# Opening a fused kernel with one unit's inverse instead of two, weight splits in 16 groups, and joint layers parted by weight halves

## The chip, the cores and the metric

The kernel runs on one core of a Trainium2 chip. The metric is device time in microseconds of one execution. The engines of a core run their own instruction streams in order and wait for each other by semaphores: TensorE (PE, with its weight loads shown apart as PEld), VectorE (DVE), ScalarE (ACT), GpSimd (POOL) and SyncE (SP), whose queue issues most of the DMAs.

## The reference

Two things are computed one after the other. For 4 batches x 8 heads, a delta-rule attention over 768 steps with head size 48, and then a feed-forward layer with a squared ReLU on the 3072 x 384 result:

```python
for t in range(S):
    y[:, :, t] = np.einsum('bhd,bhde->bhe', q[:, :, t], state)
    v_old = np.einsum('bhde,bhd->bhe', state, kt)       # kt: normalized k of step t
    state = state + bt[:, :, :, None] * np.einsum('bhd,bhe->bhde', kt, vt - v_old)
...
h = np.maximum(x @ w_in, 0.0)                           # w_in 384 x 2048
return (h * h @ w_out).astype(np.float32)               # w_out 2048 x 384
```

The weights arrive as 64-bit floats, two 32-bit words for each.

## The kernel before, in words

The work is cut into 12 units of 128 time steps x 2 batches (`units`). A unit's attention is blocked: two chunks of 64 steps, of which each needs the inverse of a triangular matrix. For most units that inverse is made on VectorE by `invert` (32 steps of two operations, L363 and L366, on blocks brought there through DRAM by the DMAs of L328 and L335), and goes back through DRAM into `tt` (L375 to L384). `static` (L280) does transposes (L301) and products (L311) with masks (L320); `whole`, `applied` (L592) and `sequential` (L616) do the rest of a unit's attention. Its output `y` is fed to the layers by `feed` (L662) as a high and a low part.

`layers` (L694) takes the 2048 hidden columns in 8 pairs (`fp`) per unit of 256 tokens: two halves of 9 matmuls (L735), the activation on ScalarE (L742 to L745), a subtraction for the low part on VectorE (L704), and later two halves of 6 matmuls (L717). A generator `yield`s after each half, so a unit's layers are 32 steps and a few more.

Every weight must first be turned from a 64-bit float into two float32r parts: `fetch` loads it, `split_weights` scales the upper word on ScalarE (L147) and combines the words by six VectorE operations (L154 to L171), or, in the first `SUMS` parts, by four operations and three matmuls (`low`, L177). There are 28 parts: 12 of `w_in` with 512 columns and 16 of `w_out` with 384, in the order of use. The working tiles come from `spool`'s `a` and `rest` with two buffers, and from `mpool`'s.

Units 0 and 1 are opened together by `first_pair` (L386): beta through `betas` and `sides`, blocks next to the diagonal by `near`, a solve of 15 double steps on VectorE for both units at once (`solve`, L472 to L505), and then products on PE that join the halves (`inner`, `joined`, `outer`, `last`). The order of instructions is written out by hand (`manual_schedule`): first this opening with pieces of the splits in between, then for each u from 1 to 11 a period, in which `weave` merges generators by given fractions of the period: `loads` (for unit u + 2: k, q, beta, normalization; for u + 1: v), `static` of unit u + 1, `state_part` of unit u, `invert` of unit u + 1, and the layers of unit u - 1. The layers of units 0 and 1 are one generator, `joint`: first half of the weights for unit 0, both halves for unit 1, second half for unit 0; unit 0's partial sums wait in `kept`, a buffer of `vt`. Of its steps, 50 lie in period 1 and the rest in period 2.

Of the kernel before, what the change touches and what calls it, by code (L numbers as in the profile page):

```python
# [20 lines left out]
def kernel(  # L21
# [25 lines left out]
    P = 128  # L47
# [28 lines left out]
    eye = spool.tile([P, 512], F32, name="a")[:, :P]  # L76
# [19 lines left out]
    ttile = []  # L96

    def new_tt():
        tt = apool.tile([P, NU, NC, H, C], F32, name="tt", bufs=1)
        ttile[:] = [tt[:, i] for i in range(NU)]  # L100
        return tt
# [13 lines left out]
    EACH = PC // P  # L115
    weight_parts = []
    for part in range(DF // PC):
        weight_parts += [("wi", (kt, part), w_in[kt * P:(kt + 1) * P, part * PC:(part + 1) * PC]) for kt in range(KT)]
        weight_parts += [("wo", ft, w_out[ft * P:(ft + 1) * P]) for ft in range(part * EACH, (part + 1) * EACH)]
    NW = len(weight_parts)  # L120
    place = [f"w{x}" for x in range(NW)]
    raws = []
    halves = {}

    rooms = [(spool, "a", "rest"), (mpool, "r", "h_l")]
    AHEAD, SUMS = 10, 6

    def fetch(n):
        for _ in range(n):
            x = len(raws)  # L130
            if x < NW:
                src = weight_parts[x][2]
                raw = wpool.tile([P, src.shape[1], 2], I32, name=place[x])
                nc.sync.dma_start(out=raw.rearrange("p a b -> p (a b)"), in_=src.bitcast(I32))
                raws.append(raw)

    def split_weights():
        started = []

        def begin():  # L140

            x = len(started)
            if x < NW:
                n = raws[x].shape[1]
                pool, first, second = rooms[x % 2 if x < AHEAD else 0]
                a, rest = [pool.tile([P, PC], I32, name=name)[:, :n] for name in (first, second)]
                nc.scalar.activation(out=a.bitcast(F32), in_=raws[x][:, :, 1].bitcast(F32), func=AF.Abs, scale=DOWN)  # L147
                started.append((a, rest))

        def words(x, sums):  # L150
            a, rest = started[x]
            n = a.shape[1]
            w0, w1 = [raws[x][:, :, i] for i in range(2)]
            nc.vector.tensor_scalar(out=a, in0=a, scalar1=3, scalar2=0 if sums else 1,  # L154
# [3 lines left out]
            if sums:  # L158
# [3 lines left out]
                hl = wpool.tile([P, 2, n], F32R, name=place[x])  # L162
            else:
# [4 lines left out]
                hl = wpool.tile([P, 2, n], F32R, name=place[x])  # L168
                power = apool.tile([P, PC], I32, name="t1", bufs=1)[:, :n]
# [3 lines left out]
            nc.scalar.copy(out=hl[:, 0], in_=a.bitcast(F32))  # L173
            halves[weight_parts[x][:2]] = hl[:, 0], hl[:, 1]
            return a, rest, hl

        def low(a, rest, hl):  # L177
            turn[1] += 1
            ps = ps_o.tile([P, PC], F32, name=f"o{turn[1] % 2}")[:, :hl.shape[2]]
            nc.tensor.matmul(ps, lhsT=ident, rhs=a.bitcast(F32), start=True, stop=False)  # L180
            nc.tensor.matmul(ps, lhsT=minus, rhs=hl[:, 0], start=False, stop=False)
            nc.tensor.matmul(ps, lhsT=plus, rhs=rest.bitcast(F32R), start=False, stop=True)
            nc.scalar.copy(out=hl[:, 1], in_=ps)

        before = None
        begin()
        begin()
        yield
        for x in range(NW):
            sums = x < SUMS  # L190
            now = words(x, sums)
            if before:
                low(*before)
            before = now if sums else None
            if x + 2 < AHEAD:
                begin()
            if x >= AHEAD - 3:
                yield
            if x + 2 >= AHEAD:
                begin()  # L200
            yield

# [14 lines left out]
    def load(u):  # L217
        t0, b0 = (u // NU) * P, (u % NU) * 2
        d = dict(u=u, t0=t0, b0=b0, y=[None] * NC, marks={})
        d["kp"] = kpad[u % 3]  # L220
        load_to(d["kp"], k, d, D, (nc.sync, nc.scalar) if u <= 1 else None)
        return d
# [21 lines left out]
    def normalize(*ds):  # L244
# [4 lines left out]
        for i in range(n):  # L249
            for c in range(NC):  # L250
                h = slice(c * H, (c + 1) * H)

                sq = (apool.tile([P, H, D], F32, name="r", bufs=2) if ds[0]["u"] in (2, 3) else
                      spool.tile([P, PC], F32, name="rest")[:, :H * D].rearrange("p (h e) -> p h e", h=H))
# [18 lines left out]
    def x_tile(u=2):  # L273

        turn[0] += 1
        pool, name = (ps_h, "h") if u <= 1 and turn[0] % 4 >= 2 else (ps_x, "x")
# [69 lines left out]
    def invert(d):  # L346
# [22 lines left out]
        if d["u"] == 2:  # L369
            tt = new_tt()  # L370
            for rows in (slice(HB, C), slice(C + HB, P)):
                nc.gpsimd.memset(tt[rows, :, :, :, :HB], 0.0)
# [3 lines left out]
        rows = ttile[d["u"] % 2].rearrange("p c h t -> p (c h) t")  # L376
# [9 lines left out]
    def first_pair(ds):  # L386


        HS = HB // 2
        NX = NC * NP  # L390
        quarter = [slice(n * HB, (n + 1) * HB) for n in range(4)]
        upper, lower = quarter[::2], quarter[1::2]
        chs = [(c, 2 * p + j, j, c * NP + p) for c in range(NC) for p in range(NP) for j in range(2)]
        made, ttall = {}, new_tt()

        def unit(i, t):
            return ttall[:, i, :, :, t].rearrange("p c h t -> p (c h) t")

        def betas():
            raw = apool.tile([P, P], F32, name="tmp", bufs=1)  # L400
            for j in range(2):
                for i, d in enumerate(ds):
                    at = (j * 2 + i) * NX
                    for r in range(2):
                        src = beta[d["b0"] + (r ^ j), j::2, d["t0"]:d["t0"] + P].rearrange("p (c t) -> c p t", c=NC)
                        nc.gpsimd.dma_start(out=raw[at:at + NX, r * C:(r + 1) * C], in_=src)
            for d in ds:
                d["kq"] = apool.tile([P, NC, NP, 2, 2, C], F32, name="kq", bufs=2)
                d["ap"] = apool.tile([P, NC, H, 2, C], F32, name="ap", bufs=2)
            z = apool.tile([P, 2, HS, HS], F32, name="z", bufs=1)  # L410
            nc.gpsimd.memset(z, 0.0)
            nc.gpsimd.affine_select(out=z, in_=z, pattern=[[0, 2], [1, HS], [-1, HS]], base=0, channel_multiplier=0,
                                    compare_op=ALU.not_equal, fill=1.0)
            made.update(raw=raw, z=z)

        def sides():
            flat = apool.tile([P, 2, 2 * NX, 2], F32, name="b0", bufs=1)
            across = apool.tile([P, 2, 2, HS], F32, name="b1", bufs=1)
            bt = apool.tile([P, 2, HS], F32, name="btp", bufs=1)
            out_ = apool.tile([P, 2, 2, HS], F32, name="sides", bufs=1)  # L420
            ps = ps_g.tile([P, 2, PC], F32, name="g")[:, 0, :HB]
            nc.tensor.transpose(ps, made["raw"][:HB], ident[:HB, :HB])
            nc.scalar.copy(out=flat, in_=ps.rearrange("p (j x) -> p j x", j=2).unsqueeze(3).broadcast_to(list(flat.shape)))
            yield
            nc.vector.transpose(out=across.rearrange("p j e s -> p (j e s)"), in_=flat.rearrange("p j x e -> p (j x e)"))
            nc.vector.tensor_scalar(out=bt, in0=across[:, :, 0], scalar1=parity[:, 0:1], scalar2=None, op0=ALU.mult)
            nc.vector.scalar_tensor_tensor(out=bt, in0=across[:, :, 1], scalar=parity[:, 1:2], op0=ALU.mult, op1=ALU.add,
                                           in1=bt)
            for e in range(2):
                nc.vector.tensor_scalar(out=out_[:, e], in0=bt, scalar1=parity[:, e:e + 1], scalar2=None, op0=ALU.mult)  # L430
            made.update(bt=bt, sides=out_)
            yield

        def transposed(i, which):
            d = ds[i]
            for c in range(NC):
                tp = x_tile(0).rearrange("p (n t) -> p n t", n=NP)
                for p in range(NP):
                    src = d["qp" if which else "kp"][:, c, 2 * p:2 * p + 2]
                    nc.tensor.transpose(tp[:, p], src.rearrange("p a b -> p (a b)"), ident)  # L440
                nc.scalar.copy(out=d["kq"][:, c, :, :, which], in_=tp.rearrange("p n (b t) -> p n b t", b=2))

        def near(i):

# [532 lines left out]
```

## Time and profile before

| | |
|---|---|
| median of 3 runs | 703.14 us (702.07 to 704.07) |
| profiled execution | 701.87 us, span 700.1 us |
| mean granted TensorE clock | 0.930 |
| PE busy | 627.3 us, 90% of the span |
| PE weight loads | 591.9 us, 85% |
| VectorE busy | 437.3 us, 62% |
| ScalarE busy | 327.6 us, 47% |
| GpSimd busy | 38.9 us, 6% |
| DMA | 47.67 MB, mean 68 GB/s |

Busy times are means over stages that have different limits, so the shares alone do not name the bound. The rows below give the engine's name, the line of the kernel, the operation, the tile written and the tiles read, and times in us from the start of the span; `SPq` is time in the issue queue of SP.

### The profile page before, as it was taken

To read this page: it belongs to the slowest core of one execution; us is meant where nothing else is said; L and a number is where in the kernel's file an instruction comes from. 1 tells how busy PE (TensorE), PEld (TensorE's weight loads), DVE (VectorE), ACT (ScalarE), POOL (GpSimd) and SP (SyncE) were. 2 spreads that over 40 slices of the span, in tenths; PEclk is the share of its full clock that TensorE was granted. 3 is DMA by queue.
4 is the path that set the end of the run, shared out by engine and by line. 5 is a ranking of instruction groups with operands and counts; after the bars stand their busy time and mean duration, and the time that the engine had idled before them with its cause. 6 is when DMAs were issued, how large, how long until landed. Compare 5 with 4: busy or idle time off the path is not lost.

```text
span 700.1 us, 24612 instructions
## 1 busy us (share of the span) xinstructions
PE 627.3 (90%) x10657; PEld 591.9 (85%) x10657; DVE 437.3 (62%) x1193; ACT 327.6 (47%) x606; POOL 38.9 (6%) x65
## 2 busy tenths in 40 slices
PE   2729759789784999999999999999999999999997
PEld 2527749788773899999999999999999999999997
DVE  5777777899476359367477576494684774651211
ACT  4705636545331454454544545535535445354352
POOL 5002300001100100100101001001001000000000
PEclk9955658989996899999999999999999999999999
DMA  7893200320332341441532423414415315020100
GB/s 181 269 365 60 38 2 2 71 44 1 54 77 47 66 87 29 91 78 28 104 59 34 99 49 46 101 34 74 90 20 111 65 23 102 11 49 16 23 2 23
DMA packets 163692, 47.67 MB, mean 68 GB/s; under 512 B 155632, under 2 KB 158720, under 8 KB 163584
## 3 DMA queue, kind: packets, MB, share of 16 engines
q1 hardware_dynamic: 160992, 45.48, 30.8%
q8 instruction: 84, 1.38, 0.8%
q10 hardware_dynamic: 2336, 0.59, 0.4%
q14 instruction: 24, 0.20, 0.1%
q0 software_dynamic: 256, 0.02, 0.0%
HBM read 36.01 MB, written 9.96 MB: 66 GB/s over the span
## 4 chain that ended last, share of the span: by engine, by line
PE 73%; DVE 14%; SPq 5%; issue 3%; DMA 2%; ACT 2%; DVEq 0%; ACTq 0%
PE h L735 27%; PE o L717 26%; SPq L215 4%; PE g L633 3%; PE g L609 2%; DVE tmp L363 2%; DVE z L366 2%; PE x L301 2%; PE x L646 2%; PE g L301 2%; PE x L311 1%; PE x L602 1%; PE g L311 1%; PE g L654 1%; DVE rest L166 1%
## 5 line engine op out<-in xcount | busy, mean ns | idle before, releaser
L717 PE MATMUL o<-w,h_h 128*128 128x384 f32 x768 | 203.6, 346 | 6.4 <-ACT vt L763 6.4
L735 PE MATMUL h<-x_h,w 128*128 128x256 f32 x1056 | 160.4, 288 | 1.5 <-ACT x_h L670 0.9
L704 DVE TENSOR_TENSOR h_l<-r,h_h 128x512 fp32r<-128x512 f32 x96 | 66.2, 689 | 141.7 <-PE o L717 67.7
L735 PEld LDWEIGHTS h<-x_h,w 128*128 128x128 f32 x1056 | 141.6, 191 | 6.9 <-issue 1.8
L717 PEld LDWEIGHTS o<-w,h_h 128*128 128x128 f32 x768 | 133.4, 190 | 8.9 <-ACT vt L763 6.6
L742 ACT ACTIVATE r<-h 128x512 f32<-128x512 f32 x96 | 57.4, 598 | 164.9 <-PE h L735 158.4
L717 PE MATMUL o<-w,h_l 128*128 128x384 f32 x384 | 130.3, 339 | 1.3 <-DVE h_l L704 1.3
L363 DVE SCALAR_TENSOR_TENSOR tmp<-lt,bt,z 128x126 f32<-128x126 f32 (+22 forms) x310 | 95.7, 309 | 29.2 <-DMA lt<-blocks 11.8
L735 PE MATMUL h<-x_l,w 128*128 128x256 f32 x528 | 91.6, 282 | 0.0
L366 DVE TENSOR_TENSOR z<-z,tmp 128x126 f32<-128x126 f32 (+22 forms) x310 | 79.2, 256 | 10.6
L735 PEld LDWEIGHTS h<-x_l,w 128*128 128x128 f32 x528 | 75.7, 191 | 0.0
L717 PEld LDWEIGHTS o<-w,h_l 128*128 128x128 f32 x384 | 72.8, 190 | 2.2 <-DVE h_l L704 2.2
L743 ACT ACTIVATE r<-r 128x512 f32<-128x512 f32 x96 | 60.8, 633 | 3.1
L745 ACT CAST h_h<-r 128x512 fp32r<-128x512 f32 x96 | 59.7, 622 | 3.1
L633 PEld LDWEIGHTS g<-state,kq 48*64 48x64 f32 x1408 | 23.5, 138 | 8.7 <-issue 2.8
L633 PE MATMUL g<-state,kq 48*64 48x48 f32 x1408 | 26.2, 224 | 4.5 <-DVE state L649 2.4
L173 ACT CAST w<-a 128x384 fp32r<-128x384 f32 (+1 forms) x23 | 12.8, 556 | 35.0 <-DVE rest L166 34.0
L588 ACT ACTIVATE tt<-x 32x256 f32<-32x256 f32 x40 | 15.0, 376 | 26.1 <-PE x L584 25.6
L354 POOL MEMSET z<- 128x512 f32 x10 | 5.4, 536 | 391.5 <-DMA inv<-z 391.4
L609 PE MATMUL g<-vt,tt 64*64 64x48 f32 x768 | 26.4, 225 | 0.3 <-ACT y L657 0.2
L609 PEld LDWEIGHTS g<-vt,tt 64*64 64x64 f32 x768 | 25.5, 142 | 0.5 <-ACT y L657 0.3
L256 DVE TENSOR_REDUCE n<-rest 128x8 f32<-128x384 f32 x20 | 10.9, 549 | 24.0 <-ACT rest L255 24.0
(193 smaller groups left out, 766.5 us busy)
## 6 DMA issues: line engine op xcount, KB each, us to landing
w<-in_moe_w_in_dram SPq DMA_DIRECT2D x12, 512.0 KB
w<-in_moe_w_out_dram SPq DMA_DIRECT2D x16, 384.0 KB
lt<-blocks SPq DMA_DIRECT2D x20, 256.0 KB
vt<-in_v_dram SPq DMA_DIRECT2D x96, 48.0 KB
kpad<-in_k_dram SPq DMA_DIRECT2D x88, 48.0 KB
qpad<-in_q_dram SPq DMA_DIRECT2D x88, 48.0 KB
out_dram<-a SPq DMA_DIRECT2D x42, 96.0 KB
blocks<-ap SPq DMA_DIRECT2D x40, 64.0 KB
```

Of the source, the lines that this page charges most:

```text
L215: queue.dma_start(out=dst[rows, c, j::2, :width], in_=src[:, c, j::2])
L301: nc.tensor.transpose(tp[:, p], src[:, c, 2 * p:2 * p + 2].rearrange("p a b -> p (a b)"), ident)
L363: nc.vector.scalar_tensor_tensor(out=tmp, in0=lt[:, s:s + 1, s + 1:].broadcast_to([P, nj, nt]), scalar=bt[:, s:s + 1], op0=ALU.mult, op1=A ...
L366: nc.vector.tensor_tensor(out=z[:, :nj, s + 1:], in0=z[:, :nj, s + 1:], in1=tmp, op=ALU.subtract)
L609: nc.tensor.matmul(g[rows, c, h], lhsT=tt[rows, c, h], rhs=vt[rows, c, h], start=True, stop=True)
L633: nc.tensor.matmul(dst[to * C:(to + 1) * C, j, p], lhsT=kq[rows, c, p, b, x], rhs=s[rows, b, p], start=(x == 0 and p == 0), stop=False, sk ...
L704: nc.vector.tensor_tensor(out=h_l, in0=r, in1=h_h.bitcast(F32), op=ALU.subtract)
L717: nc.tensor.matmul(o[i], lhsT=a[:, e, i * P:(i + 1) * P], rhs=halves["wo", ft][w], start=(begins and e == 0 and n == 0), stop=(bool(end) a ...
L735: nc.tensor.matmul(hp[:, e], lhsT=halves["wi", (kt, ft // EACH)][w][:, f], rhs=x[:, kt], start=(n == 0), stop=(n == 3 * KT - 1))
L742: nc.scalar.activation(out=r, in_=hp, func=AF.Relu)
L743: nc.scalar.activation(out=r, in_=r, func=AF.Square)
L745: nc.scalar.copy(out=h_h, in_=r)
```

## The change

- Weights come in 16 groups of 768 columns (`GC`): per 512 hidden columns two groups of `w_in` and two of `w_out`. Each group has two loads. The scaling is done in place on the upper word; `a` and `rest` have one buffer, and only group 1 uses other tiles (`x_h`, `x_l`). `SUMS` is 4 groups. Four groups are split before the layers begin, seven in period 1, five in period 2.
- `first_pair` is taken apart into functions of one unit. Unit 0 goes through its opening alone; unit 1's transposes, blocks and the solve up to its sides are put between, and the rest of its attention (`other`) is woven into the first half of period 1. The masks of the two units' products move from POOL to VectorE (`masked`). `applied` leaves out the first chunk's product for units 0 and 1.
- The loads of v for units 0 and 1 are issued among the first weights. `normalize` of unit 2 moves into period 1.
- `tt` is one tile per unit parity; `stash` keeps unit 0's `y` in `tt1`.
- `joint` now goes: unit 0 first weight half, unit 1 first half, unit 1 second half, unit 0 second half; unit 0 is fed twice, and its partial sums are stored to DRAM (`part`) and loaded back. 32 steps lie in period 1, 36 in period 2.
- Some fractions of periods 1 to 3 change, those of later periods do not.

The core of the diff:

```diff
+    GC = 768
+        weight_parts.append([(kt, ..., ("wi", part, kt, f), n) for kt, f, n in ((0, 0, 4), (1, 0, 2))])
+        weight_parts.append([(kt, ..., ("wi", part, kt, f), n) for kt, f, n in ((1, 2, 2), (2, 0, 4))])
+        for e in range(2):
+            fts = [part * EACH + 2 * e + i for i in range(2)]
+            weight_parts.append([(ft, w_out[ft * P:(ft + 1) * P], ("wo", ft), 1) for ft in fts])
+    SUMS = 4
...
+        def words(g, sums):
+            pool, first, second = (mpool, "x_h", "x_l") if g == 1 else (spool, "a", "rest")
+            a, rest = [pool.tile([P, GC], I32, name=name, bufs=1) for name in (first, second)]
...
+        for g in range(NG):
+            sums = g < SUMS
+            if g + 1 < NG:
+                scale(g + 1)
+            now = words(g, sums)
+            yield
+            if sums:
+                low(*now)
                 yield
...
+    def solve(d):          # one unit: 256 columns where both units had 512
...
+        for s in range(HS - 1):
+            nj, nt = s + 1, HS - 1 - s
...
+            if s in (4, 9):
+                yield
+        yield
...            # sides and the transpose into tt; yield; transpose into turned; yield
+    def masked(d):
+        part = d["ap"][:, :, :, 1].rearrange("p c h t -> p (c h) t")
+        nc.vector.tensor_tensor(out=part, in0=part, in1=mask[:, 1].unsqueeze(1).broadcast_to([P, H2, C]), op=ALU.mult)
...
     def results(d, o, kept=None):
+        done = kept or [spool.tile([P, GC], F32, name=n, bufs=1)[:, :DM] for n in ("a", "rest")]
...
+    def joint(d0, d1):
+        part = dram.tile([2, P, DM], F32, name="part")
         def keep(o):
+            done = [spool.tile([P, GC], F32, name=n, bufs=1)[:, :DM] for n in ("a", "rest")]
+            nc.scalar.copy(out=done[0], in_=o[0])
+            nc.vector.tensor_copy(out=done[1], in_=o[1])
+            for c in range(2):
+                nc.sync.dma_start(out=part[c], in_=done[c])
             yield
+        def back():
+            kept = [spool.tile([P, GC], F32, name=n, bufs=1)[:, :DM] for n in ("a", "rest")]
+            for c in range(2):
+                nc.sync.dma_start(out=kept[c], in_=part[c])
+            return kept
+        a, b = list(range(FT // 4)), list(range(FT // 4, FT // 2))
+        return layers([(d0, a, True, keep), (d1, a, True, None), (None, b, False, lambda o: results(d1, o)),
+                       (d0, b, True, lambda o, kept: results(d0, o, kept), back)])
...
+    def other(d, s1):      # inner, joined, halves_done and outer, last and masked, applied and stash, sequential
...
+        s0, s1 = solve(d0), solve(d1)
+        take(s0, 1)
+        transposed(d1, 0)
+        near(d1)
+        take(s0, 1)
+        transposed(d0, 1)
+        take(products(d0))
+        take(s0, 2)
+        inner(d0)
+        take(s0)
...            # joined to masked of unit 0, a split after each; loads of unit 2; applied
+        q0, p1 = sequential(d0), products(d1)
+        take(s1, 1)
+        take(q0, 2)
...
+        both = joint(d0, d1)
+        take(both, 2)
+        take(splits, 2)
...
+        at = {1: (0.66, 1.1), 2: (0.55, 1.25)}
+            if u == 1:
+                parts += [(splits, 4, 0, 0.26, "quiet"), (splits, 4, 0.32, 0.95, "quiet"), (second_norm, 6, 0.1, 0.38, "quiet")]
+            if u == 2:
+                parts += [(splits, 6, 0, 0.25, "quiet")]
+            parts += [(getting, 2, *((0.62, 0.74) if u == 1 else L1), "quiet"), (getting, 6, *N1, "quiet")]
+            if u == 1:
+                parts.append((other(d1, s1), 10, 0.0, 0.5))
+                parts.append((static(ds_[u + 1]), 2, *((0.42, 0.6) if u == 1 else A1)))
+                parts.append((state_part(ds_[u]), 7, *((0.52, 0.98) if u == 3 else Q1)))
+                parts.append((inverse, n_i, i0, min(1, i1), "quiet"))
             if u == 1:
+                parts.append((both, 32, M0, M1, ""))
             elif u == 2:
+                parts.append((both, 36, 0, M1, ""))
```

More of the change, by code (lines that the diff above doesn't have):

```diff
@@ new lines, in transposed, with near @@
+    def transposed(d, which):
+        for c in range(NC):
+            tp = x_tile(0).rearrange("p (n t) -> p n t", n=NP)
+            for p in range(NP):
+                src = d["qp" if which else "kp"][:, c, 2 * p:2 * p + 2]
+                nc.tensor.transpose(tp[:, p], src.rearrange("p a b -> p (a b)"), ident)
+            nc.scalar.copy(out=d["kq"][:, c, :, :, which], in_=tp.rearrange("p n (b t) -> p n b t", b=2))
+    def near(d):
+        ps = [x_tile(0)[:, :NX * HB].rearrange("p (x t) -> p x t", t=HB) for _ in range(2)]
+        for x in range(NX):
+            for half in range(2):
+                for r in range(2):
+                    for j in range(2):
+                        block = d["kq"][j * C:j * C + D, x // NP, x % NP, r, 0, half * HB:(half + 1) * HB]
+                        nc.tensor.matmul(ps[j][quarter[2 * r + half], x], lhsT=block, rhs=block, start=True, stop=True)
+        d["gs"] = gs = mpool.tile([P, H2, HB], F32, name="h_l", bufs=2)
+        for j in range(2):
+            nc.scalar.copy(out=gs[:, j * NX:(j + 1) * NX], in_=ps[j])
@@ new lines, in inner, with joined @@
+    def inner(d):
+        ps = x_tile(0)[:, :H2 * HS].rearrange("p (m t) -> p m t", t=HS)
+        for c, h, m in chs:
+            for rows in quarter:
+                nc.tensor.matmul(ps[rows, m], lhsT=d["gs"][rows, m], rhs=d["T"](rows, c, h, slice(HS, HB)), start=True, stop=True)
+        d["ys"] = mpool.tile([P, H2, HS], F32, name="h_h", bufs=3)
+        nc.scalar.copy(out=d["ys"], in_=ps)
+    def joined(d):
+        d["ps"] = ps = x_tile(0)[:, :H2 * HS].rearrange("p (m t) -> p m t", t=HS)
+        for c, h, m in chs:
+            for rows in quarter:
+                part = slice(rows.start, rows.start + HS)
+                nc.tensor.matmul(ps[rows, m], lhsT=d["turned"][part, m], rhs=d["ys"][part, m], start=True, stop=True)
@@ new lines, in last @@
+    def last(d):
+        ps = x_tile(0).rearrange("p (m t) -> p m t", t=HB)
+        for m in range(H2):
+            for rows in upper:
+                nc.tensor.matmul(ps[rows, m], lhsT=d["t1"][rows, m], rhs=d["m"][rows, m], start=True, stop=True)
+        for rows in upper:
+            nc.scalar.mul(out=ttile[d["u"]][rows, :, HB:], in_=ps[rows], mul=-1.0)
+    def masked(d):
+        part = d["ap"][:, :, :, 1].rearrange("p c h t -> p (c h) t")
+        nc.vector.tensor_tensor(out=part, in0=part, in1=mask[:, 1].unsqueeze(1).broadcast_to([P, H2, C]), op=ALU.mult)
@@ L694, in layers @@
     def layers(runs):
-        work = [(run, fp) for run in range(len(runs)) for fp in runs[run][2]]
-        later, o = [], []
+        work = [(run, fp) for run in range(len(runs)) for fp in runs[run][1]]
+        later, o, xs = [], [], []
         def rest():
@@ L722, in second @@
             if end and fp == fps[-1]:
-                yield from end(list(o))
+                yield from end(list(o), *ready)
         waiting = []
         for run, fp in work:
-            x_h, x_l = runs[run][1]
+            d, fps = runs[run][:2]
+            if d is not None and fp == fps[0]:
+                xs[:] = [mpool.tile([P, KT, 2 * P], F32R, name=n, bufs=1) for n in ("x_h", "x_l")]
+                yield from feed(d, xs)
+                if waiting:
+                    yield from second(*waiting.pop(0))
+            x_h, x_l = xs
             hp = ps_h.tile([P, PC], F32, name="h").rearrange("p (e t) -> p e t", e=2)
@@ L828, with both_of @@
                mybir.EngineType.Pool}
-    def piece():
-        take(splits, 1 if len(halves) < AHEAD - 3 else 2)
+    def other(d, s1):
+        take(s1, 1)
+        inner(d)
+        yield
+        take(s1)
+        joined(d)
+        yield
+        halves_done(d)
+        outer(d)
+        yield
+        last(d)
+        masked(d)
+        yield
+        for _ in applied(d):
+            stash(ds_[0])
+            yield
+        yield from sequential(d)
+    def both_of(*gens):
+        for gen in gens:
+            yield from gen
     with tc.manual_schedule(engines=engines):
@@ L910 @@
-        kept = apool.tile([P, 2, DM], F32, name="vt", bufs=2)
+        a0 = applied(d0)
+        take(a0)
+        take(splits, 1)
+        q0, p1 = sequential(d0), products(d1)
+        take(s1, 1)
+        take(q0, 2)
+        take(p1, 1)
+        take(s1, 1)
+        take(q0, 1)
+        take(s1, 1)
+        take(q0, 1)
+        take(p1)
+        both = joint(d0, d1)
+        take(both, 2)
+        take(splits, 2)
+        flags["early"] = False
         before = inverse = None
-        both = joint(*ds_[:2], x0, x1, kept)
```

514 lines of the change are left out of this document (191 added, 323 removed).

## The prediction, made before the changed kernel ran

> **What bounds the kernel now.** I read the page of the profile first: the span, the busy tenths and the granted clock.
>
> ```profile
> span 700.1 us, 24612 instructions
> ...
> PE   2729759789784999999999999999999999999997
> ...
> DVE  5777777899476359367477576494684774651211
> ...
> PEclk9955658989996899999999999999999999999999
> ```
>
> TensorE (PE) is full from the fourteenth of 40 slices on (17.5 us each, so from about 230 us). Everything before that is a head in which PE has holes and a low clock. The table of stages gives the head in numbers: PE, PE weight loads, VectorE (DVE), ScalarE (ACT) and GpSimd (POOL) busy, granted clock, DMA share.
>
> ```profile
> 27.30:44.30 17.00, 6.37 (x150) 5.09 (x148) 15.61 (x42) 7.84 (x16) 0.00 (x0) 0.75 0.99 374
> 44.30:106.00 61.70, 45.01 (x1425) 38.73 (x1425) 47.68 (x96) 28.21 (x56) 10.11 (x11) 0.58 0.28 71
> 106.00:178.50 72.50, 61.79 (x464) 59.99 (x464) 62.50 (x162) 40.41 (x73) 1.89 (x2) 0.92 0.15 28
> 178.50:229.50 51.00, 36.77 (x711) 33.38 (x711) 29.26 (x91) 15.36 (x30) 1.96 (x3) 0.81 0.33 62
> 229.50:278.00 48.50, 48.50 (x826) 46.40 (x827) 29.87 (x89) 21.62 (x40) 2.39 (x3) 0.96 0.37 65
> ```
>
> Up to 178.5 us VectorE is the busy engine (62.50 of 72.50 in period 1, the weave of u = 1). In period 2 neither engine is full. From 229.5 PE is 100% busy. The chain in order of time shows the corners, and the beat of the full part.
>
> ```profile
> 106.00 2.29 PE h L735 x9
> ...
> 179.47 1.97 PE x L301 x8
> ...
> 223.97 1.09 DMA bt<-in_beta_dram
> ...
> 226.21 1.72 PE g L301 x8
> ...
> 229.46 4.21 PE h L735 x18
> ...
> 252.43 1.09 PE x L602 x64
> ...
> 300.96 1.09 PE x L602 x64
> ...
> 670.14 2.12 PE h L735 x18
> 672.26 2.12 PE o L717 x12
> ```
>
> And one row of SP's timeline:
>
> ```profile
> 213.44 5.21 SPq L215 DMA_DIRECT2D vt<-in_v_dram  x8
> ```
>
> The layers start at 106.00. Period 1 ends about 179; in period 2 the loads of v and q for later units leave only at 213.44 (v waits for a `vt` buffer, of which `kept` holds one) and PE waits for them until 225. From 229.46 on nothing but PE counts, one unit every 300.96 - 252.43 = 48.53 us. A unit's layers are 8 pairs x (2.12 + 2.12) = 33.9 us, in 32 steps of 1.06, so attention takes 48.5 - 33.9 = 14.6 us of PE per unit. The change touches only what comes before that beat. So the time follows from one number: when the layers of unit 2 begin (229.46 now); each us there is one at the end.
>
> **The change part by part.**
>
> *Weight splits.* A part of 512 or 384 columns becomes a group of 768. VectorE's timeline gives the price, start to start: first two exact sums parts, then one part of 512 and one of 384.
>
> ```profile
> 14.23 0.42 DVE L154 TENSOR_SCALAR a<-a 128x512 int32<-128x512 int32 x1
> ...
> 16.49 0.42 DVE L154 TENSOR_SCALAR r<-r 128x512 int32<-128x512 int32 x1
> ...
> 63.72 0.39 DVE L154 TENSOR_SCALAR a<-a 128x512 int32<-128x512 int32 x1
> ...
> 66.94 0.42 DVE L154 TENSOR_SCALAR r<-r 128x512 int32<-128x512 int32 x1
> ...
> 77.40 0.35 DVE L154 TENSOR_SCALAR a<-a 128x384 int32<-128x384 int32 x1
> ...
> 79.99 0.35 DVE L649 TENSOR_TENSOR state<-state,x 128x192 f32<-128x192 f32 x1
> ```
>
> Three groups of the page serve for the rest of VectorE's work (x310 is ten inverses of 31 steps):
>
> ```profile
> L704 DVE TENSOR_TENSOR h_l<-r,h_h 128x512 fp32r<-128x512 f32 x96 | 66.2, 689 | 141.7 <-PE o L717 67.7
> ...
> L363 DVE SCALAR_TENSOR_TENSOR tmp<-lt,bt,z 128x126 f32<-128x126 f32 (+22 forms) x310 | 95.7, 309 | 29.2 <-DMA lt<-blocks 11.8
> ...
> L366 DVE TENSOR_TENSOR z<-z,tmp 128x126 f32<-128x126 f32 (+22 forms) x310 | 79.2, 256 | 10.6
> ```
>
> Six operations on 512 columns: 66.94 - 63.72 = 3.22 us; on 384: 79.99 - 77.40 = 2.59. The slope gives 4.5 us for 768, and two thirds of that, 3.0, for a sums group (2.26 at 512). All 16 groups: 4 x 3.0 + 12 x 4.5 = 66 us against 6 x 2 + 9 x 3.2 + 13 x 2.6 = 75 before: 9 us less VectorE. Against that: two solves instead of one wide one (+6, below), `masked` on VectorE where POOL had it (2 x 1.3, 1024 columns at L704's 0.69 for 512), a second feed of unit 0 (1). VectorE's sum is thus nearly what it was, and the change is one of order: only 4 of 16 groups are split ahead of the layers, where 16 of 28 parts were.
>
> *The start.* The present solve:
>
> ```profile
> 12.49 1.83 DVE L269 TENSOR_TENSOR kpad<-kpad,s 128x768 f32<-128x768 f32 x2
> ...
> 27.29 2.02 DVE L476 STREAM_TRANSPOSE lt<-vt 128x512 f32<-128x512 f32 x2 [2.91 <-ACT vt L458]
> ...
> 31.53 0.19 DVE L487 TENSOR_TENSOR tmp<-lt,z 128x30 f32<-128x30 f32 x1 [0.19 <-DVE lt L482]
> ...
> 40.20 1.03 DVE L497 TENSOR_TENSOR h_h<-z,sides 128x256 f32<-128x256 f32 x2
> 41.27 1.04 DVE L500 STREAM_TRANSPOSE tt<-h_h 128x512 f32<-128x512 f32 x1
> ```
>
> Unit 0 alone skips the four sums parts (9 us) and the other unit's blocks ahead of L476: I place its solve at 16. One transpose 1.0, three operations of half width 1.2 (2.2 for full width, 29.3 to 31.5), 30 operations at 0.24 (8.7 / 30 = 0.29 at twice the elements, 0.19 the smallest) = 7.2, sides and transpose 2.1: its inverse stands at 27.5, where both stood at 44.3. From there to the first layer VectorE does three sums groups (9), unit 1's solve up to its sides (9.4), and 6 of small work: 24 us. At the share that it reached in 44.3 to 106 (47.68 / 61.70 = 0.77) that is 31 us: the layers can start at **59**, where it is 106. Bounds: 24 us of pure work (52), and 24 plus all the idle of the stage before, 14 (66). Skipping the first chunk in `applied` saves half of L602's 1.09 per unit, on PE, and I leave it out.
>
> *Period 1, opening.* Group 3 (3), unit 1's sides and transposes (3), a wait for `low` of group 3 on PE, which holds the now single `a` and `rest` (3), then groups 4 and 5 and 2 of small work: 20 us. Step 5 of the layers needs group 5, so PE stands at **79**. From here PE has the work: 12 layer steps (12.7), unit 1's applied and sequential parts, two feeds and `static` of unit 2 (13 of the 14.6), 2 of waits: 27.6, at the clock 0.92 of the present period 1: 30, to **109**. Then `static`'s masks on VectorE (2.4).
>
> *The parked half.* `keep` now writes its two tiles to DRAM through SP, from `a` and `rest`, which group 9 needs next. SP's rows of now show what will stand ahead of it, and the price of an issue:
>
> ```profile
> 126.74 1.98 SPq L328 DMA_DIRECT2D blocks<-ap  x4
> 130.23 1.15 SPq L335 DMA_DIRECT2D lt<-blocks  x2
> 131.43 6.54 SPq L215 DMA_DIRECT2D kpad<-in_k_dram  x8
> 138.07 5.21 SPq L215 DMA_DIRECT2D vt<-in_v_dram  x8
> ```
>
> The sixteen loads of v that move ahead of most weights, and four more weight issues, cost SP some 13 us at these 0.65 each. The late groups are split late, which hides it; without that cover groups 4 to 7 would stop VectorE.
>
> `blocks`, `lt` and the loads k and v of the first `getting` item (at 0.65 of the period; `keep` is layer step 23, at 0.69, group 9 at 0.714) take 143.28 - 126.74 = 16.5 us after the masks; two issues of the parked half 1.3; its landing 2 by the nearest row, a store of such tiles:
>
> ```profile
> 195.66 1.94 DMA out_dram<-a
> ```
>
> So group 9 can't begin before 111.4 + 19.8 = **131**. VectorE has 10 to 11 us of other work meanwhile (group 8 4.5, inverse steps, one L704, the copy) and then stands for 9. Bounds: nothing, if VectorE comes later than I think, and 20, if all that work is behind.
>
> *To the last split that binds.* Groups 9 to 13 (22.4), the 27 remaining inverse steps at 0.31 + 0.26 and gaps (16.7 with the last product), normalization of unit 3 (3), four L704 (2.6): 45 us, to **176**. Step 40 of the layers (the eighth of period 2) needs group 13. Behind it lie 26 computing steps (27.6), unit 2's attention without `static` (10), and two last steps (2.1): 40 us of PE, to **216**. v and q of later units are not late there: no `kept` holds a `vt` buffer any more. Unit 3's `static` and the feed then take 229.46 - 226.21 = 3.3 from its second eight transposes on, and 2.0 for the first eight: 5.3. One cost more: at about 0.69 of period 2 the Square of unit 4 writes `a`, which unit 1's result stores still read; 0 to 4.4 us of ACT (four issues and a landing), I take 1.5 since PE has steps in hand. The layers of unit 2 begin at 216 + 5.3 + 1.5 = **223**.
>
> *The clock.* The stage 44.3 to 106 ran at a granted 0.58, period 1 at 0.92. The Trainium skill, "TensorE: Matmul & The Clock Gate", section "Why this matters for your kernels", says that PE gaps of over about 3 us between bursts put the clock back to half. By that rule, the stretch from 79 to 109 runs cold as it comes after stops of 5 us; the trace agrees in that the stage with PE's holes has 0.58. What this would make of the time is the first rival.
>
> **The sum.** 229.5 - 223 = 6.5 us off a span of 700.1: 693.6. The profiled execution took 701.87, 1.8 over its span, and the median of the runs is 1.3 above that: 695.4 by its own scale, **697** by the median.
>
> **The rivals.**
>
> *PE stays cold in period 1 (slower).* For: the stage before the layers had 0.58 with PE 73% busy, and the new period 1 holds about 46 us of PE work in over 90. Against: period 1 now has 0.92 with gaps too. At 0.58 the 27.6 us take 47.6 instead of 30: +17.6, that is 11 slower than now, **714**. It decides from a clock of about 0.76 (27.6 / 36.5).
>
> *The order gives back what the start gains (no change).* VectorE's work is as large as before, and every stop of it up to group 13 counts in full; from 59 to 131 lie 72 us with 45 of work (groups 3 to 8, unit 1's rest, normalization of unit 2, which moves in here, and masks), so I count 27 us of stops already, and 6.5 more level it. For it: the wait of PE on its own instruction stream in the same steps, which my sum doesn't contain:
>
> ```profile
> PE x L512 <- issue: 4.0, 1, 4.0
> ```
>
> Then **703**.
>
> *The parked half waits for nothing.* If SP's loads are out before `keep`, the stop of 9 goes, and with a start at 55 the gain is 6.5 + 9 + 4 = 19: **684**; against it, SP's order has both loads ahead.
>
> *The start slips.* If unit 0's small matmuls wait for instructions and loads (DMA share 0.99 in 27.3 to 44.3), the layers start at 72, not 59: **710**.
>
> **How the numbers follow.** The forecast, 690 to 700 around 697: 0.35. The parked half free, 680 to 690: 0.20. Level, 701 to 705: 0.15. Cold PE, 706 to 720: 0.20. A slipped start, 706 to 714: 0.10. Faster by over 0.3% (2.1 us, about what a measurement of this kernel can tell): 0.55; within: 0.15; slower: 0.30. Cutting one tenth at each end gives 684 to 714.
>
> **What would show it.** The first L735 near 59; group 9's first operation after a VectorE stop of about 9 us, released by the store of the parked half; PE stops before layer steps 5 and 40, released by VectorE; PE full from about 176; unit 2's layers at 223; the same 48.5 us beat behind. A period 1 with a clock under 0.76, a first layer after 66, or a beat that is longer than 48.5 (the stores from `a` and `rest` holding the Squares in every period) would make the prediction wrong.

## The result, and the profile after

The changed kernel takes 742.97 us (median of 4 runs, 742.55 to 744.05), the kernel before 703.4 in the same comparison: a ratio of 1.0567, with a 95% interval of 1.0548 to 1.0587. The forecast was 697, its range 684 to 714. The times of the experiments below are medians of four runs, but for e14, of which one run took 1250.41 us and the other three are used. Line numbers below are those of the changed kernel: L710 and L687 are the matmuls of the layers (before: L735 and L717), L153 begins the split of a group. In runs that edit a line above them they stand one line higher or lower (L709 or L711 for L710).

From the page: the span, and the busy tenths in 40 slices, which are now 18.6 us long.

```profile
span 742.3 us, 24458 instructions
PE   3485787723769599999999999999999999999997
DVE  5665536609993484755847748467576494661211
PEclk9677668965679799999999999999999999999999
```

PE is full only from the fifteenth slice on (about 260 us), and in VectorE's row the ninth slice (148 to 167 us) is a 0. The table of stages has the columns of the one shown before (PE, PE loads, DVE, ACT, POOL busy, granted clock, DMA share, GB/s).

```profile
27.30:44.30 17.00, 9.68 (x328) 7.59 (x328) 9.84 (x13) 3.64 (x7) 0.15 (x1) 0.54 0.73 185
44.30:106.00 61.70, 44.78 (x970) 37.75 (x971) 34.11 (x72) 29.72 (x53) 6.02 (x9) 0.72 0.41 129
106.00:178.50 72.50, 43.10 (x490) 40.38 (x486) 38.06 (x87) 23.44 (x39) 0.00 (x0) 0.79 0.17 34
178.50:229.50 51.00, 33.58 (x335) 30.74 (x336) 44.06 (x84) 19.77 (x33) 3.94 (x5) 0.70 0.21 37
229.50:278.00 48.50, 38.87 (x645) 36.84 (x643) 28.71 (x89) 18.04 (x33) 0.00 (x0) 0.89 0.23 48
```

VectorE, which in the head before was a little busier than PE (62.50 and 61.79 of 72.50 us in period 1), works 38.06 us in that stage. Neither engine is full in any of the stages ahead of 229.5: most of the head is made of waits. The one stretch that VectorE fills is 165.2 to 208.5, where it splits groups 9 to 13 (40.82 of 43.30 us busy). The corners of the head, from the timelines of PE and VectorE (start, duration, in brackets the idle time ahead and what ended it):

```profile
80.41 0.87 PE L710 MATMUL h<-x_h,w 128*128 128x256 f32 x6
96.62 1.22 PE L710 MATMUL h<-x_h,w 128*128 128x256 f32 x4 [3.10 <-ACT w L167]
134.40 0.68 DVE L321 TENSOR_TENSOR ap<-g,mask 128x512 f32<-128x512 f32 x1
165.21 0.56 DVE L153 TENSOR_SCALAR a<-w 128x768 int32<-128x768 int32 x1 [16.73 <-DMA part<-a]
208.50 0.55 DVE L153 TENSOR_SCALAR a<-w 128x768 int32<-128x768 int32 x1
269.31 0.98 PE L710 MATMUL h<-x_h,w 128*128 128x256 f32 x6 [1.22 <-ACT x_h L647]
391.08 2.03 PE L586 MATMUL g<-vt,tt 64*64 64x48 f32 x64
439.82 2.03 PE L586 MATMUL g<-vt,tt 64*64 64x48 f32 x64
```

In this order: the first layer step, the fifth (the first that needs groups 4 and 5; two of its matmuls run before this row), the last mask of `static` of unit 2, group 9 behind the parked half, the end of group 13 (the next group starts), and the layers of unit 2, at 269.31 where they were at 229.46: 39.85 us later. The last two rows are the beat, 48.74 (before 48.53); over the periods that follow it adds some 2 us, and 39.85 + 2 is the 42.2 by which the spans differ.

Two stops explain themselves in these views. SP's timeline between the masks and group 9:

```profile
135.11 1.99 SPq L329 DMA_DIRECT2D blocks<-ap  x4
138.64 1.15 SPq L336 DMA_DIRECT2D lt<-blocks  x2
139.83 5.34 SPq L214 DMA_DIRECT2D kpad<-in_k_dram  x8
145.28 5.21 SPq L214 DMA_DIRECT2D vt<-in_v_dram  x8
150.59 5.24 SPq L214 DMA_DIRECT2D qpad<-in_q_dram  x8
155.88 5.32 SPq L238 DMA_DIRECT2D bt<-in_beta_dram  x8
162.46 0.55 SPq L239 DMA_DIRECT2D bt<-bt  x1
163.07 0.57 SPq L741 DMA_DIRECT2D part<-a  x1
163.68 0.43 SPq L741 DMA_DIRECT2D part<-rest  x1
```

The parked half's stores are the last two rows: they stand behind 33 load issues, at 0.65 us each, and VectorE waits 16.73 us for `a`. And in period 2, from the waits of ACT, DVE and PE, and behind them the row of SP's timeline that belongs there:

```profile
ACT a L256 <- DMA out_dram<-a: 12.3, 1, 12.3
DVE n L257 <- ACT a L256: 9.1, 1, 9.1
PE g L610 <- DVE state L626: 8.3, 1, 8.3
```

```profile
248.12 1.23 SPq L663 DMA_DIRECT2D out_dram<-a  x2
```

The Square of unit 4 writes `a`, which waits for unit 1's result stores; these too stand behind 33 loads on SP. Behind the Square waits its sum on VectorE, behind that an update of unit 2's state, and behind that PE: one wait in a queue, handed on twice.

The third loss, before 97 us, has no single row. These are the longest waits of VectorE between 27.3 and 80.6:

```profile
DVE tt L508 <- PE x L504: 6.6, 1, 6.6
DVE a L153 <- ACT w L189: 4.7, 1, 4.7
DVE x_l L648 <- ACT x_h L647: 3.7, 1, 3.7
```

### The profile page after: what moved, and what is told of

Same layout as the page of the kernel before. It is cut to its first block, busy times and chain, and to the rows that moved or that the text cites. A ratio compares the mean times of both kernels' runs of the same rounds, so it can differ in the third digit from the quotient of the medians.

```text
span 742.3 us, 24458 instructions
## 1 busy us (share of the span) xinstructions
PE 638.5 (86%) x10607; PEld 600.3 (81%) x10607; DVE 436.3 (59%) x1168; ACT 325.9 (44%) x591; POOL 34.6 (5%) x63
## 4 chain that ended last, share of the span: by engine, by line
PE 69%; DVE 11%; SPq 7%; DMA 7%; ACT 3%; issue 2%; DVEq 0%; ACTq 0%
PE h L710 25%; PE o L687 24%; DMA w<-in_moe_w_in_dram 4%; SPq L214 4%; PE g L610 3%; PE g L586 3%; SPq L238 2%; PE x L579 2%; DVE tmp L364 2%; DVE a L155 1%; SPq L140 1%; DMA kpad<-in_k_dram 1%; DVE rest L164 1%; DVE z L367 1%; PE x L312 1%
## 5 line engine op out<-in xcount | busy, mean ns | idle before, releaser
L687 PE MATMUL o<-w,h_h 128*128 128x384 f32 x768 | 208.2, 353 | 4.3 <-DVE rest L739 3.2
L710 PE MATMUL h<-x_h,w 128*128 128x256 f32 x1152 | 180.2, 293 | 26.9 <-ACT r L717 17.0
L710 PEld LDWEIGHTS h<-x_h,w 128*128 128x128 f32 x1152 | 159.2, 195 | 33.4 <-ACT r L717 17.3
L675 DVE TENSOR_TENSOR h_l<-r,h_h 128x512 fp32r<-128x512 f32 x96 | 66.4, 692 | 155.2 <-PE o L687 79.3
L687 PEld LDWEIGHTS o<-w,h_h 128*128 128x128 f32 x768 | 136.6, 195 | 7.4 <-DVE rest L739 3.6
L687 PE MATMUL o<-w,h_l 128*128 128x384 f32 x384 | 132.4, 345 | 0.0
L717 ACT ACTIVATE r<-h 128x512 f32<-128x512 f32 x96 | 57.4, 598 | 168.0 <-PE h L710 167.8
L710 PE MATMUL h<-x_l,w 128*128 128x256 f32 x576 | 102.6, 287 | 0.0
L710 PEld LDWEIGHTS h<-x_l,w 128*128 128x128 f32 x576 | 84.8, 194 | 0.1
L687 PEld LDWEIGHTS o<-w,h_l 128*128 128x128 f32 x384 | 74.4, 194 | 0.0
L167 ACT CAST w<-a 128x768 fp32r<-128x768 f32 x15 | 12.5, 830 | 63.4 <-DVE rest L164 62.0
L610 PEld LDWEIGHTS g<-state,kq 48*64 48x64 f32 x1408 | 23.6, 138 | 15.4 <-ACT y L634 10.2
L610 PE MATMUL g<-state,kq 48*64 48x48 f32 x1408 | 26.5, 224 | 11.0 <-DVE state L626 8.3
L647 ACT CAST x_h<-h 128x384 fp32r<-128x384 f32 x26 | 12.4, 481 | 32.0 <-PE h L645 32.0
L586 PE MATMUL g<-vt,tt 64*64 64x48 f32 x768 | 24.4, 218 | 0.0
```

Of the source, the lines that this page charges most:

```text
L586: nc.tensor.matmul(g[rows, c, h], lhsT=d["T"](rows, c, h), rhs=vt[rows, c, h], start=True, stop=True)
L610: nc.tensor.matmul(dst[to * C:(to + 1) * C, j, p], lhsT=kq[rows, c, p, b, x], rhs=s[rows, b, p], start=(x == 0 and p == 0), stop=False, sk ...
L675: nc.vector.tensor_tensor(out=h_l, in0=r, in1=h_h.bitcast(F32), op=ALU.subtract)
L687: nc.tensor.matmul(o[i], lhsT=a[:, e, i * P:(i + 1) * P], rhs=halves["wo", ft][w], start=(begins and e == 0 and n == 0), stop=(end is not ...
L710: nc.tensor.matmul(hp[:, e], lhsT=halves["wi", ft // EACH, kt, ft % EACH][w], rhs=x[:, kt], start=(n == 0), stop=(n == 3 * KT - 1))
L717: nc.scalar.activation(out=r, in_=hp, func=AF.Relu)
```

## The experiments

The theory: three losses in turn, (A) a late start, (B) the parked half behind loads on SP, (C) the result stores behind loads on SP. Rivals: what one wait gives back another takes; a cold TensorE; VectorE's total. Ratios are to the kernel before, with 95% intervals.

**e1, e2, e3: the two stores.** In e1 `keep` issues its stores from ScalarE; in e2 unit 4's Squares use other buffers; e3 does both.

```
-                nc.sync.dma_start(out=part[c], in_=done[c])
+                nc.scalar.dma_start(out=part[c], in_=done[c])      # e1, e3
-  sq = (apool.tile([P, H, D], F32, name="r", bufs=2) if ds[0]["u"] in (2, 3) else
+  sq = (apool.tile([P, H, D], F32, name="r", bufs=2) if ds[0]["u"] in (2, 3, 4) else   # e2, e3
```

> Changed kernel, but the two stores of the parked half are issued by ScalarE instead of SyncE; nothing else moves. Theory (three waits in turn: a late start, the parked half behind 33 loads on SyncE, the result stores behind 33 loads): VectorE's stop of 16.73 us ahead of group 9 is gone, group 9 starts at 148 to 150 instead of 165.2, and since groups 9 to 13 are VectorE's work the layers of unit 2 begin 13 to 17 us earlier: about 728. Rival (what one wait gives back another takes: the loads or the Squares of unit 4 stop the same engines later): less than 6 us, 737 to 743. Rival (period 1 is slow because TensorE is cold there): no change, the mean granted clock between 106 and 178 stays at 0.79.

> Changed kernel, but the two Squares of unit 4 write the buffers r of the attention pool, as those of units 2 and 3 do, instead of rest and a. Theory (three waits): ScalarE no longer stands 12.3 us for the result stores of unit 1, VectorE not 9.1 for the Square, TensorE not 8.3 for the state: 7 to 9 us off, about 735. Rival (TensorE has other work or the k loads are late there in any case): within 2 us of 743.

> Both edits at once: parked half stored by ScalarE, Squares of unit 4 in r. Theory (three waits, one behind the other, so they add): 20 to 26 us off, 717 to 723, still 14 to 20 over the kernel before, which is the late start. Rival (one takes what the other gives): no more than the larger of the two alone, about 728.

Measured: e1 726.16 us (1.0339, 1.0314 to 1.0364), e2 732.63 (1.0428, 1.0391 to 1.0465), e3 716.48 (1.0194, 1.0167 to 1.0220). Off the changed kernel that is 16.8, 10.3 and 26.5 us; 16.8 + 10.3 = 27.1, so they add. In e1's timelines the store leaves from ScalarE as soon as the copy is done, and group 9 has no stop ahead of it:

```profile
137.19 0.36 ACTq L741 DMA_DIRECT2D part<-a  x1
144.71 0.55 DVE L153 TENSOR_SCALAR a<-w 128x768 int32<-128x768 int32 x1
```

(B) and (C) are shown, and the rival that another wait takes the gain falls. What remains of e3 over the kernel before, 13.5 us, is put down to (A). Its corners fit that: the fifth layer step runs at 95.44, 16.4 us later than predicted, and the layers of unit 2 begin at 241.40, 18.4 later than predicted, so the start is most of what is left; behind it the prediction's terms nearly cancel in e3 (PE's stretch 6 us longer than said, the wait for group 9 6.5 shorter).

One thing has to be kept in mind for all that follows on the start. The changed kernel, e1, e2 and e3 have the same instructions ahead of the layers, and in their traces the first layer step begins at 80.41, 76.98, 78.89 and 79.91, because stops of PE that the profile puts down to nothing it shows ("issue") differ: ahead of the last matmuls of L504 they are 3.4, 1.7, 1.2 and 3.1 us. A difference of 3 us at the start between two traces therefore needs no edit; the medians and their intervals decide.

**e4: the sums groups.** `SUMS = 0`, with the first four groups' yields kept, so that the order stays.

> Changed kernel, but the first four groups are split by six VectorE operations like the others, at the same places of the order; the six TensorE matmuls and two ScalarE copies of each sums group are gone. Theory (at the start the sums groups cost stops, but VectorE pays nearly as much for splitting them itself: 4 x 1.5 more against stops of 2.15, 1.73 and 4.69): the first matmul of the layers at 76 to 80 instead of 80.6, the time 0 to 4 us shorter. Rival (the sums groups on a slow TensorE are most of the late start): the first layer before 70, 10 us off. Rival (VectorE's total decides the head): 6 us longer.

Measured: 738.95 (1.0509, 1.0486 to 1.0533), 4.0 off. The time came as the theory had it, the way there did not: the first layer step begins at 72.88, earlier than said, but then VectorE stands 6.8 us for the activation behind the first two steps, and the fifth comes at 93.53, only 3.1 before the 96.62 of the changed kernel. VectorE's total goes up by 4.6 us by the page (440.9 against 436.3) and the time down, so that rival falls; the small matmuls are a part of the late start and not most of it.

**e5, e7: another order.** On e3. Groups 4 and 5 and three layer steps ahead of unit 1's sides; e7 with e4's edit as well. The counts in period 1's weave are lowered to match.

```
         take(both, 2)
-        take(splits, 2)
+        take(splits, 5)
+        take(both, 3)
```

> The kernel of e3 with another order at the head: groups 4 and 5 and three layer steps of unit 0 stand ahead of unit 1's sides, transposes and small matmuls, instead of behind them. Theory (the late start is VectorE coming late to group 5): group 5 begins near 82 instead of 89 and the fourth layer step runs near 87 instead of 96; period 1 ends 6 to 9 us earlier, time 708 to 711. Rival (unit 1's own chain of small matmuls and copies sets the end of period 1, and it now starts 14 us later): static's masks after 138 instead of 132.7, time 720 to 728.

> The kernel of e5 with all groups split by six VectorE operations, so that group 4 does not wait for the TensorE matmuls and ScalarE copies of group 3. Theory (late start, in which those waits are 4 to 6 us): 3 to 5 under e5. Rival (VectorE's total decides): 4 to 6 over e5.

Measured: e5 718.07 (1.0212, 1.0184 to 1.0239), 1.6 over e3, so no gain; e7 712.02 (1.0116, 1.0083 to 1.0150), 6.0 under e5. From e5's timeline of VectorE:

```profile
81.57 0.55 DVE L153 TENSOR_SCALAR a<-w 128x768 int32<-128x768 int32 x1
89.00 1.03 DVE L484 STREAM_TRANSPOSE tt<-h_h 128x512 f32<-128x512 f32 x1
134.05 1.29 DVE L321 TENSOR_TENSOR ap<-x,mask 128x512 f32<-128x512 f32 x2 [7.40 <-PE x L312]
```

Group 5 begins 7.5 us earlier than in e3 (89.07), but unit 1's transpose (89.00) comes 15.4 us after e3's 73.56, and `static`'s masks at 134.05 instead of 131.45. So both halves of my expectation were half right: the split was late, and once it comes early, unit 1's chain of small matmuls, copies and waits holds the masks up.

**e6: later weights.** On e3. Groups 8 to 15 are loaded behind unit 2's loads.

```
-        fetch(NG)
...
         load_beta(ds_[2])
+        fetch(NG)
```

> The kernel of e3 with the loads of weight groups 8 to 15 issued behind the loads k, q and beta of unit 2 (from about 80 us on) instead of ahead of them (40 to 57). Theory (TensorE's waits on its own instruction stream, 2.1 + 3.4 + 1.4 + 1.4 us between 27 and 80, come from sharing the DMA engines with the weights): they shrink to under 3 in sum and the layers start 4 to 6 us earlier, time 711 to 713. Rival (weights and streams do not meet): the waits stay, time within 2 of 716.5. Rival (groups 8 and 9 come late from DRAM): slower than 718.

Measured: 711.34 (1.0114, 1.0085 to 1.0142), 5.1 under e3. The time is as expected and the intervals lie apart, the reason is shown only in part: the two longest issue stops of PE stay at 3.6 and 1.8 us (e3: 3.1 and 2.1), and only the two shorter ones (1.8 and 1.1) fall under 0.9. VectorE's wait on the feed, 3.9 us in e3, is 0.9.

**e9, e12: both edits of the start, and one of them.** e9 is e6 with `SUMS = 0`; e12 is e3 with `SUMS = 0`.

> The kernel of e3 with both edits of the start: all groups by six VectorE operations (no small matmuls and copies for the first four) and weight groups 8 to 15 loaded behind unit 2's loads; order of the start as in the changed kernel. Theory (the late start is several waits in a row and they add): 716.5 - 4.0 (e4) - 5.1 (e6) = 707, with the first matmul of the layers near 73. Rival (they overlap: e6 already took the waits that the small matmuls cause): 710 to 711. Under 702 would mean that the new order gains once its waits are gone.

> The kernel of e3 with all groups split by six VectorE operations; the weights loaded early, as in the changed kernel. It is e9 without the later weights. Theory (the 719 of e9 came from the late weights: its DMA engines are full from 68 to 86 us, and TensorE, at the first layer there, waits 4.6 and 3.1 us for its own instructions): 712 to 713 here, that is e3's 716.5 less the 4.0 that the same edit took off the changed kernel, and no wait on its instructions at the first layer. Rival (dropping the small matmuls leaves TensorE idle and at half clock, and the layers start cold): 717 to 720, as e9.

Measured: e9 719.06 (1.0222, 1.0186 to 1.0257), a miss by 12; e12 714.95 (1.0160, 1.0130 to 1.0191), between what theory and rival had said and 1.5 under e3 with overlapping intervals. Two rows of e6 and then two of e9, 68 to 76 and 76 to 84 us, the waits of PE in e9 (70 to 95), and the second layer step in e9 and in e12:

```profile
68.00:76.00 8.00, 5.19 (x135) 3.96 (x136) 3.58 (x5) 1.68 (x3) 0.00 (x0) 0.57 0.50 148
76.00:84.00 8.00, 5.12 (x158) 4.74 (x156) 5.09 (x8) 4.28 (x7) 0.00 (x0) 1.00 1.02 393
```

```profile
68.00:76.00 8.00, 4.12 (x137) 3.79 (x137) 7.86 (x11) 0.70 (x2) 0.00 (x0) 0.50 0.95 326
76.00:84.00 8.00, 1.90 (x128) 1.79 (x128) 0.06 (x1) 0.00 (x0) 0.00 (x0) 0.50 1.04 405
```

```profile
PE h L709 <- issue: 4.6, 1, 4.6
PE x L503 <- issue: 2.5, 1, 2.5
```

```profile
84.00 1.65 PE L709 MATMUL h<-x_h,w 128*128 128x256 f32 x6 [4.57 <-issue]
```

```profile
79.29 1.65 PE L709 MATMUL h<-x_h,w 128*128 128x256 f32 x6 [1.74 <-issue]
```

In both the late weights fill the DMA engines (share 1.02 and 1.04). In e9 PE has its issue stops just then, and the engines stand: PE, VectorE and ScalarE are 1.90, 0.06 and 0 us busy out of 8. In e6 PE has no such stop there and works on. e12 is e9 with only the weights' loads moved back: the stop ahead of the second layer step is 1.74 us, at a DMA share of 0.01 (77.5 to 79.3), where e9 has 4.57 at 1.04 (79.4 to 84). So the stop is there without any weights in flight and is longer with them, and what a burst of weights costs depends on whether such a stop falls into it. That PE waits for its own instructions in these stops is a reading: the profile shows nothing that it waits for. In time e9 is 4.1 us over e12, with intervals that just touch (from 1.0186 and up to 1.0191). The edits of the start don't add.

**e10, e14, e13, e15: the clock.** e10 is e9 in e5's order. e13, e14 and e15 put extra matmuls (`busy`, 128x512 each, their result not read) into PE's waits, on e12, e10 and e12.

```
         take(s1, 1)
+        busy(14)             # e15: 30
         inner(d)
...
         halves_done(d)
+        busy(6)              # e15: 10, and 8 behind outer
         outer(d)
```

> The kernel of e9 with the order of e5 (groups 4 and 5 and three layer steps ahead of unit 1's sides). From e7 (712.0, without the later weights) less e6's 5.1: 707. Theory (unit 1's chain sets the end of period 1): no better than e9, within 2. Rival (VectorE coming late to group 5 sets it): 3 to 5 under e9.

> The kernel of e12 with 20 extra matmuls of 128x512 (their result is not read): 14 ahead of unit 1's inner matmuls, where TensorE stands 7.6 us, and 6 ahead of its outer matmuls, where it stands 2.9. Rival of the prediction, cold TensorE (in e12 the granted clock is 0.50 from 60 to 100 us and a layer step's first six matmuls take 1.65 us instead of 0.88): the clock between 72 and 100 rises to 0.9 or more, the 10 layer steps and small matmuls there shorten by 6 to 9 us, of which 4 to 7 reach the end: 708 to 711. Theory (waits for VectorE, ScalarE and the instruction stream set that stretch, the clock only fills them): clock up, time within 2 of 715.

> The kernel of e10 (711.2: six-operation splits, later weights, groups 4 and 5 and three layer steps ahead of unit 1) with the same 20 matmuls; here TensorE stands 12.9 us ahead of unit 1's inner matmuls, so the 14 fit. Cold TensorE: clock over 0.9 from 75 us on, 706 to 708. Theory of waits: 710 to 712.

> The kernel of e13 with 48 extra matmuls instead of 20: 30 ahead of unit 1's inner matmuls (at 0.25 us each they fill the 7.6 us that TensorE stands there), 10 ahead of the outer matmuls and 8 behind them. In e13 the 14 were over 4.3 us before the inner matmuls and the clock was back at 0.54 to 0.60 from 68 to 84. Cold TensorE: the first layer's six matmuls at 73 take 0.9 us instead of 1.65, the clock is over 0.85 from 64 to 92, and the time falls by 2 to 5 more, to 706 to 709. Theory of waits (what e13 gained was an instruction wait of 1.7 us and the place of the work): clock up, time 710 to 712.

Measured: e10 711.22 (1.0112, 1.0088 to 1.0137); e13 710.87 (1.0125, 1.0095 to 1.0154); e14 712.20 (1.0148, 1.0108 to 1.0188); e15 713.23 (1.0134, 1.0101 to 1.0168). The stretch 64 to 100 us of e12 and of e15:

```profile
64.00:100.00 36.00, 20.66 (x440) 19.33 (x440) 21.71 (x31) 13.01 (x21) 5.13 (x7) 0.50 0.13 20
```

```profile
64.00:100.00 36.00, 31.55 (x493) 27.35 (x494) 22.73 (x31) 13.99 (x24) 4.86 (x7) 0.79 0.13 23
```

The clock went from 0.50 to 0.79, and the first layer's six matmuls from 1.65 to 0.98 us, but the time stayed within 2 us of e12's, and the fifth layer step still waited 3.3 us for group 5 (3.1 before). What a faster PE saves there, it partly waits away, and partly the extra matmuls themselves cost it: the 30 end at 73.73, 2 us after the inner matmuls of e12 begin (71.59), so e15 is no clean price of the clock. e10 is 7.8 under e9, more than the 3 to 5 of its rival, but 4 over the 707 of its sum and level with e6 and e7; e14's matmuls end 11 us before the inner ones and change nothing. e13 is 4 us under e12, within overlapping intervals. In its trace the fifth layer step comes 3.9 us earlier (90.15 instead of 94.09), but 2.3 of these are there already at the second step (76.97 instead of 79.29), most of them e12's issue stop of 1.74, which e13 lacks; no more than the last 1.6 can be the shorter matmuls. The Trainium skill, "TensorE: Matmul & The Clock Gate", section "Why this matters for your kernels", has the clock fall back to half after gaps of over about 3 us; the rows of e12 agree (gaps of 7.6, 2.9 and 3.1 us, 0.50 throughout). What that costs in this stretch, where PE waits for others, is at most a few us by these runs.

**e8, e11: the kernel before, with the stall that its profile shows taken out.** In period 2 the load of v for unit 3 goes behind those of q and beta for unit 4; e11 also loads the last 10 of its 28 parts behind unit 2's loads, as e6 does.

> The kernel before, with the load of v for unit 3 issued behind the loads of q and beta of unit 4 in period 2, so that these no longer stand behind a transfer that waits for its buffer. From the reading of the profile before: TensorE's stops of 5.36 (for that beta) and 3.6 us ahead of unit 2's layers shrink, 4 to 8 us off: 695 to 699. Rival (v comes later and unit 3's products wait for it instead): no change, 703.

> The kernel of e8 (the kernel before, v of unit 3 loaded behind q and beta of unit 4) with the last 10 of the 28 weight parts loaded behind unit 2's loads. Theory (weights in flight slow the small matmuls of the start by 3 to 5 us, in this kernel too): 692 to 694. Rival (there VectorE is the busy engine and hides it): 695 to 698.

Measured: e8 696.46 (0.9899, 0.9871 to 0.9926), e11 693.50 (0.9877, 0.9843 to 0.9911). SP's timeline of e11:

```profile
200.22 5.24 SPq L215 DMA_DIRECT2D qpad<-in_q_dram  x8
205.51 5.35 SPq L237 DMA_DIRECT2D bt<-in_beta_dram  x8
212.74 5.54 SPq L215 DMA_DIRECT2D vt<-in_v_dram  x8
```

q and beta leave at 200 to 211, where they left from 218.69 and 223.97, and the layers of unit 2 begin at 220.62 (before 229.46). Both beat both kernels, by moving lines of the order alone. The 3 us between e8 and e11 lie within overlapping intervals.

## Why the prediction was wrong, step by step

- *What counts.* Right: the layers of unit 2 set the time (39.85 of 42.2 us), nothing behind them but 0.2 us a unit.
- *Unit 0's inverse.* Right: its transpose ends at 28.2, said 27.5.
- *The first layer at 59, step 5 at 79.* Wrong, 80.4 and 96.6. The first is partly a fault of reading: by the order, unit 1's inner matmuls and group 3's sums matmuls stand ahead of it on PE. The second is the term that was mis-sized, by 17.6: I gave VectorE 0.77 of the time, and it had 0.56 from 28.2 to 80.6 (29.46 of 52.40 us). One reason that the runs show: with `a` and `rest` single, the next split waits for the PE matmuls and the copy of the one before (4.7 us at group 4; without the sums groups, in e4, 4.0 us off). A second: weights in flight (e6: 5.1). A third is a term that the sum put at nothing, though the prediction names it: PE's issue stops of 2.1, 3.4, 1.4 and 1.4 us between 27 and 80, of which the 3.4 is half of VectorE's longest wait (6.6, for L504). Unit 1's chain is a fourth, argued from e5's trace; no run took it away.
- *PE's stretch of 30 us.* Mis-sized by 6: from 96.6 to the masks' end at 135.1 are 38.5 us, 36.1 without the masks' 2.4. PE was busy for 30.57 us of these 36.1 at a clock of 0.80, where the sum has 2 us of waits and 0.92; the 27.6 us at 0.80 would be 34.5, so the clock may be the larger part of the 6. No run tried it there.
- *The parked half.* The mechanism was right, place and releaser too; the size wasn't. I counted one item of loads ahead of the stores, k and v, and the weave takes from the same generator in two parts, so that q and beta, 17 more issues of 0.65, came first as well: 30.1 us from masks to group 9, said 19.8. In the kernel before, too, SP's next row behind the two that the prediction shows is q:

```profile
143.38 5.24 SPq L215 DMA_DIRECT2D qpad<-in_q_dram  x8
```

  So the reading stopped a row too early. e1 gives 16.8 us back, where I said a stop of 9; the 16.73 lies inside the bounds of that term, 0 to 20.
- *Groups 9 to 13.* Right: 165.2 to 208.5 are 43.3, said 45.
- *The result stores.* The place was right, the price wrong: 1.5 taken, bounded by 4.4, and it is 10.3 (e2). I priced the four issues and the landing, not what stands ahead of them on SP, though I had just done that sum for the parked half; and the wait passed from ScalarE to VectorE to PE, which I had thought to have steps in hand. The stretch from group 13 to unit 2's layers is 60.8 us, said 47; of these 13.8 the Square explains 8.8, and the other 5 stay open.
- *The sum.* 17.6 at step 5, 6.1 in PE's stretch, 10.3 at the parked half, 1.7 the other way in groups 9 to 13 and 13.8 behind them make 46.1 of the 46.3 us by which 269.3 misses 223.
- *The rivals.* Cold PE: period 1 had 0.79 in 106 to 178.5, and the stretch that the rival is about, 96.6 to 132.7, 0.80, both over the 0.76 from which it was to decide. It may cost up to 4.5 us there by the sum above, and little between 64 and 100 (e13, e15). The start that slips happened, and further than its 72. The loss goes beyond the range because the late start, the parked half and the result stores came together; my range took one change at a time, and priced the result stores at 4.4 at most.

What stays open: how the 13.5 us of (A) divide. The two edits that take a part away give 1.5 (e12, not clear of noise) and 5.1 us (e6) on e3, and together nothing (e9, 2.6 over, intervals overlapping). That an issue stop of PE falls into a burst of weights fits this, and e12, which moves the burst alone, is 4.1 under e9, but just at the edge of what the runs can tell. No median with the new plan came under 710.87 (e13).

## What to carry to other kernels

A store that frees a buffer is as late as the queue in front of it: before a tile is made single or shared, count every issue ahead of its store on that queue, from all generators that feed it, times the issue price. And follow the wait on: a ScalarE instruction that stands 12 us stops VectorE's next sum, and that stops TensorE's next matmul. Where the profile of before shows one such stall, moving a load behind others may be worth more than a new plan of the work.

## What was not expected of the hardware

TensorE stops for nothing that the profile shows, at the same place in two kernels for 1.74 us with the DMA engines idle (share 0.01, e12) and for 4.57 with weight transfers filling them (share 1.04 at 401 GB/s, e9), and all that depends on it stands. The longest such stop was 4.75 us (e7, L503, at a share of 1.02 in 32 to 38 us). A granted clock of 0.50 instead of 0.79 over 36 us (e12 and e15) went with 1.7 us of time, less than the runs can tell, in a stretch where TensorE waits for others; as e15 also runs 48 more matmuls, that is a hint and not a price.
